# Gated mix of local attention and a Mish MLP: the second half's first layer by seven products, a joined v product, and GpSimd beside small softmax steps

## The chip, the core and the metric

The kernel runs on one core of one Trainium2 chip. The metric is device microseconds (us) of that core from one launch; the time of a kernel is the median of its runs, 620.25 us for the kernel before (three runs, 619.38 to 621.33). Engines are named as in the profile: PE (matrix multiply), PEld (its weight load), DVE (vector), ACT (scalar activation), POOL (GpSimd), SP (the queue that issues most transfers).

## The reference, cut to what matters

```python
x = A_x                                              # 2048 x 640, one batch
g = sigmoid((x * gate_w).sum(-1, keepdims=True))
q, k, v = split(x @ wqkv)                            # 32 heads of 20
# token s looks at s, s-2, ..., s-14 (8 positions, masked where negative)
a = softmax(q . k_window * 20**-0.5) @ v_window @ wo
h = x @ w1 + b1                                      # 640 -> 1728
b = (h * tanh(softplus(h))) @ w2                     # Mish, then 1728 -> 640
out = g * a + (1 - g) * b
```

All inputs are float32. The kernel keeps float32 accuracy on PE by splitting each operand into a rounded high part and a low part, so that one product of blocks is three matmuls (high by high, high by low, low by high: `mm3`, L515 to L517).

## The kernel before

**Tiling.** The 2048 tokens are four blocks `tb` of 512; blocks 0 and 1 are half P = 0, blocks 2 and 3 are half P = 1. The 640 input features are five K blocks `kc` of 128. The work on PE is, in order: the q, k, v projection in eight units `u` (half P, a quarter of the heads), each with eight slots of 15 matmuls; beside it the first MLP layer in six "quads" per half, a quad being two chunks of 128 hidden features by two token blocks, so four results of 128x512; then the second MLP layer (`mlp2`) and the output projection (`wo_part`).

**Products of blocks.** The first half's quads (`Quad`) use Strassen's scheme in Winograd's form on K blocks 0 to 3 (two pairs, seven products for eight), and K block 4 plainly. The intermediate sums are kept in PSUM: ACT copies a running sum from one bank to the next (`seed`, L1147), PE goes on adding to it, and for two of the four results DVE adds a kept product (`added`, L1165) before Mish. The second half's quads in the kernel before are `Plain`: four results, five K blocks each, no such copy and no such addition. A class `Single` is in the file too, but not used before: it takes one pair of K blocks (0 and 2) by seven products and the other three plainly.

**Operands.** `pieces(P, q)` loads the weights of a quad and splits them: ACT writes the high part (L447), then POOL or DVE the low part as a difference (L450). `x_forms(P, i)` builds the four sums of input blocks that the seven products need (L1020) and splits them. `sums_of` makes the same kind of sums of the second layer's weights (L1242, L1255).

**Attention.** It runs on DVE, two slots at a time: the product of q with k (`scores`, L572, 2560 elements per partition), its sum over a head (L575), the small softmax steps on 256 elements (largest L593, difference L594, sum L606, reciprocal L607, weights L608), the product with v (`outputs`, L617, two instructions of 1280 elements), its sum (L621), a transposition (L528).

**What sets the order.** `ORDER` is a list of tokens that creates the tasks (`u.4.3` is slot 3 of unit 4, `q.1.0.m1` a step of a quad, `pieces.1.0`, `sum`); `BANKS` says from which of two rings of three PSUM banks, `qb` or `sb`, a result takes its bank. A planner (`Plan.run`, L106) then walks through time with a cost for each task and writes each engine's instructions in the order that it finds; on the chip each engine runs its list in that order and waits on semaphores. For DVE and POOL it has a rule: POOL starts a task that can wait only while DVE runs a "quiet" one, and while POOL reads, DVE starts only quiet ones (`QUIET`, L72). Quiet are the large attention steps and tasks of kind `psum`. Before, the small softmax steps have no kind and so aren't quiet. Tasks marked "ANY" go to POOL or DVE, whichever the planner finds first.

Of the kernel before, what the change touches and what calls it, by code (L numbers as in the profile page):

```python
# [254 lines left out]
ORDER = """
u.0.5 u.0.7 u.0.6 pieces.0.1 q.0.0.first u.0.4 q.0.1.first q.0.0.second q.0.0.m1 q.0.0.m3 last.0 q.0.0.m4 q.0.1.m1 q.0.1.second q.0.1.m4 wq.1 q.0.0.m2
q.0.1.m3 last.1 q.0.0.l2 q.0.1.l2 u.1.1 q.0.0.l1 u.1.0 u.1.2 q.0.1.m2 u.1.3 u.1.4 u.1.7 pieces.0.2 q.0.1.l1 sum u.1.5 q.0.2.first q.0.2.m1 u.1.6
q.0.2.second q.0.2.m3 wa.2 p.2.1.a1 p.2.0.a1 q.0.2.m4 p.2.0.a2 pieces.0.3 sum q.0.2.m2 q.0.2.l2 p.2.1.a2 p.2.0.a3 p.2.0.b2 p.2.0.b1 p.2.1.a3 q.0.2.l1
p.2.2.a1 p.2.1.b1 p.2.2.a2 p.2.2.a3 p.2.2.b2 pieces.0.4 p.2.1.b2 p.2.3.a1 p.2.3.a2 p.2.2.b1 p.2.3.b1 p.2.3.a3 p.2.1.c0 wc.2 p.2.3.b2 x.3.4 q.0.3.first
p.2.0.c0 q.0.3.m1 q.0.3.second q.0.3.m3 q.0.3.m4 pieces.0.5 q.0.4.second q.0.3.l1 x.2.2 x.2.1 x.3.1 p.2.3.c0 q.0.3.m2 x.3.0 q.0.4.first q.0.3.l2  # L260
q.0.4.m1 p.2.2.c0 q.0.4.m3 q.0.4.m4 q.0.4.m2 q.0.4.l2 x.2.3 q.0.4.l1 q.0.5.first x.3.2 p.2.3.c1 x.3.3 wq.4 q.0.5.m1 q.0.5.second p.2.3.c2 q.0.5.m4
p.2.1.c1 p.2.2.c1 p.2.0.c1 p.2.0.c3 p.2.2.c2 q.0.5.m2 p.2.0.c2 p.2.2.c3 x.2.4 x.2.0 sum p.2.3.c3 q.0.5.m3 p.2.1.c3 q.0.5.l1 p.2.1.c2 q.0.5.l2
pieces.1.0 third u.4.2 u.4.3 u.4.5 u.4.1 u.4.4 u.4.7 u.4.0 u.4.6 rest.0 q.1.0.m1 rest.1 sum sum wq.5 q.1.0.m2 sum q.1.0.second pieces.1.1 pieces.1.2
q.1.0.first u.5.2 u.5.0 sum u.5.4 wq.6 u.5.1 pieces.1.3 u.5.7 q.1.2.second q.1.1.m2 u.5.5 u.5.3 u.5.6 q.1.1.second q.1.2.first sum u.6.3 q.1.1.m1
u.6.4 q.1.1.first q.1.2.m2 q.1.3.m2 u.6.1 q.1.3.m1 u.6.2 u.6.7 u.6.5 q.1.2.m1 lastw.1 u.6.6 u.6.0 pieces.1.4 sum last.2 wq.7 q.1.3.second q.1.4.m1
u.7.5 pieces.1.5 q.1.4.first q.1.4.m2 q.1.4.second q.1.5.second last.3 q.1.3.first u.7.0 u.7.7 u.7.4 q.1.5.m2 q.1.5.m1 q.1.5.first u.7.6 u.7.2 u.7.1
u.7.3 rest.2 rest.3
# [4 lines left out]
def kernel(ctx: ExitStack, tc: tile.TileContext, x, wq, wo, w1, b1, w2, out):  # L272
# [279 lines left out]
    def attention(u, P, hq, ready, gates):  # L552
# [36 lines left out]
        def softmax(a, rank, after, used):  # L589
# [3 lines left out]
            step("DVE", 430, lambda: V.tensor_reduce(mx[:, h], lg[:, h], op=OP.max, axis=AX.X), after)  # L593
# [9 lines left out]
        def shares(a, rank, e, copied):  # L603
            h = slice(a, a + 4)
            step = chain(rank)
            t = step("DVE", 415, lambda: V.tensor_reduce(sm[:, h], lg[:, h], op=OP.add, axis=AX.X), [e])  # L606
            step("DVE", 390, lambda: V.reciprocal(sm[:, h], sm[:, h]))  # L607
            return t, step("DVE", 430, lambda: V.tensor_tensor(pg[:, h], pg[:, h], sm[:, h, None, :].to_broadcast([128, 4, W, HQ]), op=OP.mult), [copied])  # L608

        def outputs(s0, rank, after):  # L610
# [3 lines left out]
            def mul(s):  # L614
                vw = window(kv, s0, 1)
                vw = bass.AP(tensor=vw.tensor, offset=vw.offset + s * ROW, ap=[list(vw.ap[0]), [2 * ROW, W // 2], [ROW, 2], [DH, HQ], [1, DH]])
                V.tensor_tensor(pairs[:, s].rearrange("p k i (h d) -> p k i h d", d=DH), vw,  # L617
                                pg[:, s0 + s].rearrange("p (k i) h -> p k i h", i=2)[:, :, :, :, None].to_broadcast([128, W // 2, 2, HQ, DH]), op=OP.mult)
# [1347 lines left out]
```

## Time and profile before

| | before |
|---|---|
| runs, us | 619.38, 620.25, 621.33 (median 620.25) |
| span of the profiled execution, us | 617.7 |
| PE busy | 611.9 us, 99%, 2716 instructions |
| DVE busy | 580.3 us, 94%, 546 instructions |
| ACT busy | 370.0 us, 60%, 856 instructions |
| POOL busy | 316.7 us, 51%, 291 instructions |
| TensorE clock granted | 0.999 of full |

The profiled execution gives its span, from the first to the last instruction; no other time stands for it, and the median of the runs is 2.55 us above that span. Matmuls are pipelined, and the busy time of one (0.39 us) is longer than the distance from one start to the next, so a busy PE says little about short gaps; the starts in the timeline do. Names of tiles: `sb` and `qb` are PSUM banks of the two rings, `pair` a split operand, `raw` a loaded one, `hb` an activation, `pr` the attention product, `lg` and `pg` logits and weights.

### The profile page before, as it was taken

The numbers are of one execution on the slowest core, as the hardware profiler recorded it, in microseconds if no ns is written. First come the engines' busy times: TensorE is split into PE (matmuls) and PEld (weight loads), VectorE is DVE, ScalarE is ACT, GpSimd is POOL, SyncE is SP. The second block draws the span as 40 slices with busy tenths as digits, with TensorE's granted clock in tenths as the row PEclk, the third lists the DMA queues.
The fourth block names the chain that finished last, engine by engine and source line by source line (L and its number), as shares of the span: only waits on it lengthen the run. The fifth ranks groups of instructions, "written<-read, shape, count | busy, mean of one in ns | idle before, by whom it ended". The sixth has DMA issues, their size and how long they took to land.

```text
span 617.7 us, 9122 instructions
## 1 busy us (share of the span) xinstructions
PE 611.9 (99%) x2716; PEld 508.1 (82%) x2716; DVE 580.3 (94%) x546; ACT 370.0 (60%) x856; POOL 316.7 (51%) x291
## 2 busy tenths in 40 slices
PE   9999999999999999999999999999999999999997
PEld 6878888888888888888888888888888888888886
DVE  8899999999999999999999999999989999989955
ACT  7685847677796456673465455777766543565520
POOL 1665758877865555745452737788427713001000
PEclk9999999999999999999999999999999999999999
DMA  9764775899997878898966859988869864599813
GB/s 330 227 184 146 197 254 167 242 294 263 337 303 229 252 238 253 227 282 281 236 187 222 233 175 286 304 219 259 261 219 285 241 211 131 178 327 295 305 53 119
DMA packets 100769, 145.95 MB, mean 236 GB/s; under 512 B 11552, under 2 KB 54560, under 8 KB 100496
## 3 DMA queue, kind: packets, MB, share of 16 engines
q1 hardware_dynamic: 97360, 139.61, 70.5%
q0 software_dynamic: 3072, 5.51, 6.0%
q8 instruction: 21, 0.34, 0.2%
q10 hardware_dynamic: 288, 0.26, 0.1%
q14 instruction: 28, 0.23, 0.1%
HBM read 91.33 MB, written 53.03 MB: 234 GB/s over the span
## 4 chain that ended last, share of the span: by engine, by line
PE 87%; DVE 7%; ACT 2%; DMA 2%; issue 2%; SPq 0%; DVEq 0%; ACTq 0%
PE qb L516 16%; PE qb L517 16%; PE qb L515 16%; PE sb L515 12%; PE sb L516 12%; PE sb L517 12%; DVE pr L572 2%; DVE lg L575 2%; DMA act<-hb 1%; DVE pair L450 1%; DVE raw L1020 1%; PE qb L677 1%; ACT hb L1153 1%; DVE hb L1165 1%; DMA ot<-o 1%
## 5 line engine op out<-in xcount | busy, mean ns | idle before, releaser
L450 POOL TENSOR_TENSOR pair<-raw,pair 128x512 fp32r<-128x512 f32 (+4 forms) x128 | 157.1, 1247 | 111.9 <-ACT pair L447 60.3
L447 ACT ACTIVATE pair<-raw 128x512 fp32r<-128x512 f32 (+2 forms) x229 | 132.8, 606 | 66.7 <-DMA raw<-actt 20.4
L517 PE MATMUL qb<-pair 128*128 128x512 f32 (+1 forms) x403 | 155.7, 386 | 0.0
L516 PE MATMUL qb<-pair 128*128 128x512 f32 (+1 forms) x403 | 155.7, 386 | 0.0
L515 PE MATMUL qb<-pair 128*128 128x512 f32 (+1 forms) x403 | 155.7, 386 | 0.0
L515 PE MATMUL sb<-pair 128*128 128x512 f32 (+2 forms) x374 | 144.9, 388 | 0.2
L517 PE MATMUL sb<-pair 128*128 128x512 f32 (+2 forms) x374 | 144.7, 387 | 0.0
L516 PE MATMUL sb<-pair 128*128 128x512 f32 (+2 forms) x374 | 144.7, 387 | 0.0
L617 DVE TENSOR_TENSOR pr<-kvq,pg 128x1280 f32<-128x1280 f32 x64 | 93.1, 1484 | 1.0
L572 DVE TENSOR_TENSOR pr<-kvq,qg 128x2560 f32<-128x2560 f32 x32 | 89.9, 2811 | 2.4 <-ACT qg L578 1.3
L621 DVE TENSOR_REDUCE kvq<-pr 128x320 f32<-128x2560 f32 x32 | 90.2, 2818 | 0.8
L575 DVE TENSOR_REDUCE lg<-pr 128x128 f32<-128x2560 f32 x32 | 90.2, 2818 | 0.7
L515 PEld LDWEIGHTS qb<-pair 128*128 128x128 f32 x403 | 75.6, 188 | 14.8
L516 PEld LDWEIGHTS qb<-pair 128*128 128x128 f32 x403 | 75.7, 188 | 14.7
L517 PEld LDWEIGHTS qb<-pair 128*128 128x128 f32 x403 | 75.6, 188 | 14.6
L515 PEld LDWEIGHTS sb<-pair 128*128 128x128 f32 x374 | 70.2, 188 | 15.3 <-ACT sb L1147 0.5
L516 PEld LDWEIGHTS sb<-pair 128*128 128x128 f32 x374 | 70.2, 188 | 14.1
L517 PEld LDWEIGHTS sb<-pair 128*128 128x128 f32 x374 | 70.2, 188 | 14.1
L450 DVE TENSOR_TENSOR pair<-raw,pair 128x512 fp32r<-128x512 f32 (+2 forms) x101 | 70.1, 715 | 2.6 <-ACT pair L447 2.3
L1020 POOL TENSOR_TENSOR hb<-hb 128x512 f32<-128x512 f32 x39 | 50.5, 1304 | 22.0 <-ACT hb L1153 12.7
L683 ACT ACTIVATE kvq<-qb 128x320 f32<-128x320 f32 x50 | 21.8, 436 | 50.1 <-PE qb L517 49.8
L447 ACT ACTIVATE pair<-hb 128x512 fp32r<-128x512 f32 (+3 forms) x62 | 36.5, 589 | 1.5 <-PE qb L517 1.2
(164 smaller groups left out, 730.3 us busy)
## 6 DMA issues: line engine op xcount, KB each, us to landing
actt<-hb SPq DMA_DIRECT2D x52, 256.0 KB, 3.8
raw<-in_w SPq DMA_DIRECT2D x40, 256.0 KB, 3.5
act<-hb SPq DMA_DIRECT2D x38, 256.0 KB, 3.0
raw<-actt SPq DMA_DIRECT2D x37, 256.0 KB, 3.7
raw<-in_wq SPq DMA_DIRECT2D x36, 248.0 KB, 3.8
raw<-act SPq DMA_DIRECT2D x29, 256.0 KB, 3.5
raw<-in_x SPq DMA_DIRECT2D x23, 256.0 KB, 4.6
o<-ot SPq DMA_DIRECT2D x64, 80.0 KB, 1.9
```

The lines of the kernel that those rows point to most:

```text
L447: a = add("ACT", act_ns(n), lambda: A.activation(hi(), raw(), AF.Copy), after, rank=rank, take=take, hold=hold)
L450: return (V if e == "DVE" else G).tensor_tensor(lo(), raw(), hi().bitcast(F32), op=OP.subtract)
L515: nc.tensor.matmul(ps, ah, bh, start=first, stop=False, skip_group_check=more)
L516: nc.tensor.matmul(ps, ah, bl, start=False, stop=False, skip_group_check=more)
L517: nc.tensor.matmul(ps, al, bh, start=False, stop=last, skip_group_check=more)
L572: return V.tensor_tensor(pr, window(kv, s0, 0), qg[:, :, None, :].to_broadcast([128, 2, W, QF]), op=OP.mult)
L575: V.tensor_reduce(lg_w[:, s0:s0 + 2], pr.rearrange("p s w (h d) -> p s w h d", d=DH), op=OP.add, axis=AX.X)
L617: V.tensor_tensor(pairs[:, s].rearrange("p k i (h d) -> p k i h d", d=DH), vw, pg[:, s0 + s].rearrange("p (k i) h -> p k i h", i=2)[:, :, ...
L621: V.tensor_reduce(q[:, s0:s0 + 2], pairs.rearrange("p s k i f -> p s f k i"), op=OP.add, axis=AX.XY)
L677: nc.tensor.matmul(ps.t[:, :n], X[0, kc].t[:, a, i * 128:(i + 1) * 128], WQ[0, kc].t[:, b, :n], start=a == b and kc == 0, stop=False)
L683: a = add("ACT", 330, lambda: A.activation(kv[:, 7 + s], ps.t[:, QF:3 * QF].rearrange("p (a b) -> p a b", a=2), AF.Copy), [done] + before, ...
L1020: return (V if e == "DVE" else G).tensor_tensor(t.t[:, i:i + n], a.t[:, j:j + n], b.t[:, k:k + n], op=op)
```

## The change

- All six quads of the second half become `Single`: one pair of K blocks by seven products, with `pieces` in its other branch and one `x_forms` for half 1 (the token `forms.1.0`).
- The product with v is one instruction for two slots in place of two.
- The five small softmax steps, the transpositions of the attention's output and of `hx`, and the DVE additions of `mlp2` get the kind `psum`, so that the planner lets POOL work beside them.
- Only matmuls that read the six kept input blocks now hold up the third attention buffer (`x_uses`).
- `ORDER` and `BANKS` are new throughout, the first half's part too.

```diff
-KIND = 'PPPPPP'
+KIND = 'SSSSSS'
-BANKS = {'q03al': 's', 'p23be': 'q', 'p21de': 's', ...}
+BANKS = {'l0': 's', 'p20al': 's', 'p20de': 's', ...}
-u.0.5 u.0.7 u.0.6 pieces.0.1 q.0.0.first u.0.4 q.0.1.first ...
-pieces.1.0 third u.4.2 u.4.3 u.4.5 u.4.1 u.4.4 u.4.7 u.4.0 u.4.6 rest.0 q.1.0.m1 rest.1 sum sum wq.5 q.1.0.m2 sum q.1.0.second ...
+u.0.5 u.0.6 u.0.4 u.0.7 q.0.0.first last.0 wq.1 q.0.0.m1 ...
+p.2.0.c2 u.4.3 q.0.5.l1 u.4.1 u.4.5 rest.0 u.4.2 sum pieces.1.0 forms.1.0 u.4.7 u.4.6 q.1.0.first u.4.0 q.1.0.m1 wq.5 u.5.4 ...
...
-            step("DVE", 430, lambda: V.tensor_reduce(mx[:, h], lg[:, h], op=OP.max, axis=AX.X), after)
+            step("DVE", 430, lambda: V.tensor_reduce(mx[:, h], lg[:, h], op=OP.max, axis=AX.X), after, kind="psum")
...
-            step("DVE", 390, lambda: V.reciprocal(sm[:, h], sm[:, h]))
+            step("DVE", 390, lambda: V.reciprocal(sm[:, h], sm[:, h]), kind="psum")
...
-            for s in range(2):
-                step("DVE", 1495, lambda s=s: mul(s), after if not s else (), kind="pv mul")
+            step("DVE", 2760, mul, after, kind="pv mul")
...
-        x_uses.append(add("PE", *a, **k))
-        return x_uses[-1]
+        t = add("PE", *a, **k)
+        if any(b.ring is plan.rings["xh"] for b in k["hold"]):
+            x_uses.append(t)
+        return t
```

What a quad of the second half now does (`Single`, there before but not called); `plain` stands for three K blocks:

```python
def first(self):   # al <- one product;  be <- copy of al
    self.p1 = self.mms(self.al, self.one(0, 0, self.xk(0, 0)), [], [self.al], True)
    self.sb = self.seed(self.be, self.al, [self.p1])
def second(self):  # ep <- one product;  v <- copy of ep
...
def m1(self):      # be += one product;  ga <- copy of be
def m2(self):      # al += one product + plain, then Mish
def m3(self):      # be += one product + plain, then DVE adds v, then Mish
def m4(self):      # ga += one product;  de <- copy of ga
def l1(self):      # ga += plain, then DVE adds v, then Mish
def l2(self):      # de += one product + plain, then Mish
```

More of the change, by code (lines that the diff above doesn't have):

```diff
@@ L255 @@
 ORDER = """
[L256 to L267, printed above, removed]
+u.0.5 u.0.6 u.0.4 u.0.7 q.0.0.first last.0 wq.1 q.0.0.m1 q.0.0.m4 q.0.0.m2 sum q.0.0.second q.0.0.m3 pieces.0.1 u.1.0 last.1 u.1.2 q.0.0.l2
@@ new lines @@
+p.2.2.c0 q.0.4.second q.0.4.m2 q.0.4.m4 p.2.1.b2 p.2.3.c0 p.2.3.b2 q.0.4.m3 wq.4 q.0.4.l1 q.0.4.l2 q.0.5.m1 p.2.0.c1 p.2.2.c1 p.2.3.c1 q.0.5.m2
+p.2.2.c2 x.2.3 q.0.5.m4 x.2.0 q.0.5.l2 q.0.5.second p.2.3.c2 p.2.0.c3 p.2.2.c3 p.2.3.c3 p.2.1.c1 p.2.1.c3 p.2.1.c2 x.3.2 third x.3.0 x.3.4 q.0.5.m3
+p.2.0.c2 u.4.3 q.0.5.l1 u.4.1 u.4.5 rest.0 u.4.2 sum pieces.1.0 forms.1.0 u.4.7 u.4.6 q.1.0.first u.4.0 q.1.0.m1 wq.5 u.5.4 rest.1 pieces.1.1 u.5.2
+u.4.4 q.1.1.first q.1.0.second sum q.1.0.m4 u.5.1 q.1.0.m3 u.5.3 sum q.1.1.second q.1.1.m2 sum u.5.6 q.1.1.m1 pieces.1.2 u.5.0 u.5.7 q.1.1.m4 wq.6
@@ new lines @@
+q.1.0.m2 u.5.5 q.1.2.first sum q.1.0.l2 u.6.2 u.6.4 q.1.1.l2 q.1.0.l1 q.1.2.m1 q.1.1.m3 u.6.3 wq.7 u.6.1 q.1.1.l1 u.6.5 u.6.0 u.7.2 u.6.7 u.7.3 u.7.6
+q.1.2.second q.1.2.m4 sum pieces.1.3 pieces.1.4 u.6.6 sum q.1.2.m2 q.1.4.first q.1.2.m3 q.1.2.l2 u.7.5 u.7.1 q.1.3.first q.1.3.m2 u.7.4 u.7.0
+q.1.3.second pieces.1.5 q.1.2.l1 q.1.3.m1 u.7.7 q.1.4.m1 q.1.4.m4 q.1.4.m2 q.1.3.m4 q.1.3.m3 q.1.3.l2 q.1.4.second q.1.3.l1 q.1.4.l2 rest.2
+q.1.5.first q.1.4.m3 q.1.5.m1 q.1.4.l1 q.1.5.m4 q.1.5.m2 lastw.1 q.1.5.second q.1.5.m3 q.1.5.l1 q.1.5.l2 last.2 last.3 rest.3
@@ L629, in out @@
             ot = plan.buf("ot", lambda: at.tile([128, QF // 32, 4, 32], F32, name="ot"))
-            t = add("DVE", 780, lambda: turn(ot.t, q[:, s0:s0 + 4], QF // 32), after, rank=rank, take=[ot])
+            t = add("DVE", 780, lambda: turn(ot.t, q[:, s0:s0 + 4], QF // 32), after, rank=rank, take=[ot], kind="psum")
             tb = 2 * P + (s0 == 0)
@@ L749, in ended @@
             kv = KV[UNIT[u]]
-            before = sum((freed.get((BEFORE.get(u), s), []) for s in range(8)), [])
+            before = sum((freed[BEFORE[u], s] for s in range(8)), []) if u in BEFORE else []
             halo = {}
@@ L1009, in mlp1_rest @@
         t = add("DVE", 430, lambda: turn(blocks(), hx[:, P, 4 * h:4 * h + 4].rearrange("p j a b -> p j (a b)"), FR // 32),
-                hxd[P] + before, rank=SOON, take=[z, b] if P else [b], late=late)
+                hxd[P] + before, rank=SOON, take=[z, b] if P else [b], late=late, kind="psum")
         d = turned_out(lambda: h_d[tb], blocks, [t], [b], late)
@@ L1409, in run @@
                 return (V if e == "DVE" else G).tensor_tensor(out.t, a.t, b.t, op=op)
-            return add(eng, either(eng, 512), run, after, rank=rank, take=take, hold=[out, a, b])
+            return add(eng, either(eng, 512), run, after, rank=rank, take=take, hold=[out, a, b], kind="psum" if eng == "DVE" else "")
         def result(b, tb, dc, after):
```

23 lines of the change are left out of this document (14 added, 9 removed).

## Prediction

> **What bounds the kernel now.** I read the page first, then a table of busy time by stage, then the starts of PE's matmuls one by one, then the groups of the engines that feed PE. The page's head:
>
> ```profile
> span 617.7 us, 9122 instructions
> PE 611.9 (99%) x2716; PEld 508.1 (82%) x2716; DVE 580.3 (94%) x546; ACT 370.0 (60%) x856; POOL 316.7 (51%) x291
> ```
>
> PE is the bound by share, with DVE close behind. A share can hide stages, so here are the stages: start-up, first half, second half's first layer (200 to 365 us), and the two output stages. The columns are PE, PEld, DVE, ACT and POOL, then the granted clock.
>
> ```profile
> core 0: us, PE busy (x) PEld busy (x) DVE busy (x) ACT busy (x) POOL busy (x), PEclk, DMA share, GB/s
> 0.00:62.00 62.00, 60.24 (x257) 47.78 (x257) 56.27 (x57) 42.73 (x100) 31.55 (x33) 1.00 0.68 221
> 62.00:200.00 138.00, 137.87 (x616) 115.50 (x617) 133.37 (x111) 98.15 (x248) 100.68 (x89) 1.00 0.83 256
> 200.00:365.00 165.00, 165.00 (x738) 138.33 (x737) 160.46 (x109) 89.23 (x229) 88.51 (x87) 1.00 0.80 239
> 365.00:420.00 55.00, 55.00 (x246) 45.85 (x246) 53.35 (x36) 38.05 (x84) 41.51 (x36) 1.00 0.81 244
> 420.00:500.00 80.00, 80.00 (x355) 66.24 (x354) 77.25 (x85) 52.28 (x107) 43.55 (x38) 1.00 0.86 255
> ```
>
> From 62 us on, PE is visibly idle for 0.13 us in all of these stages, at full clock. In the stage that changes, DVE is at 97% (160.46 of 165), but ACT at 54% and POOL at 54%. So a matmul less is time less, as long as PE's inputs and banks keep coming in time.
>
> What one matmul costs is read from starts, since its shown duration overlaps the next:
>
> ```profile
> 599.93 0.39 PE L515 MATMUL qb<-pair 128*128 128x512 f32 x1
> ...
> 611.26 0.39 PE L517 MATMUL sb<-pair 128*128 128x512 f32 x1
> ```
>
> Here are 50 steps of 128x512 in 11.33 us: **0.2266 us** each. (The Trainium skill, "TensorE: Matmul & The Clock Gate", section "Wait — 56ns, not 53.3ns?", gives 215.7 ns for a warm 512-wide step; by it the 18 matmuls below would be worth 3.9 us, not 4.1. The trace differs from it by 5%, and the trace decides.)
>
> With that step, all the gaps on PE behind the start-up can be found by their starts. There are three worth naming. The first:
>
> ```profile
> 35.01 0.39 PE L516 MATMUL qb<-kvq,pair 128*128 128x512 f32 x1
> 36.20 0.49 PE L517 MATMUL qb<-kvq,pair 128*128 128x512 f32 x1 [0.80 <-DVE pair L450]
> 36.53 0.39 PE L515 MATMUL qb<-kvq,pair 128*128 128x512 f32 x1
> ```
>
> 1.19 and 0.33 us where 0.23 each would do: 1.06 us lost, on a split that DVE made late. The second shows how the seven products stall:
>
> ```profile
> 57.92 2.82 DVE L572 TENSOR_TENSOR pr<-kvq,qg 128x2560 f32<-128x2560 f32 x1
> 60.66 0.68 DVE L1165 TENSOR_TENSOR hb<-hb,sb 128x512 f32<-128x512 f32 x1
> 61.37 0.58 ACT L1147 ACTIVATE sb<-sb 128x512 f32<-128x512 f32 x1 [1.74 <-DVE hb L1165]
> 61.49 0.39 PE L517 MATMUL qb<-kvq,pair 128*128 128x512 f32 x1
> 62.01 0.50 PE L515 MATMUL sb<-pair 128*128 128x512 f32 x1
> 62.34 0.39 PE L516 MATMUL sb<-pair 128*128 128x512 f32 x1
> ```
>
> The addition L1165 stood behind a 2.82 us attention product, the copy L1147 waited for the addition, and PE for the copy: 0.29 + 0.10 = 0.39 us lost. The third, at 177.56 us, is of the same family (the gap is 0.50 where a 496-wide step is 0.22, then 0.33):
>
> ```profile
> 174.11 2.81 DVE L575 TENSOR_REDUCE lg<-pr 128x128 f32<-128x2560 f32 x1
> ...
> 176.84 0.67 DVE L829 TENSOR_TENSOR sb<-sb,pair 128x496 f32<-128x496 f32 x1
> ...
> 177.06 0.38 PE L517 MATMUL qb<-pair,kvq 128*128 128x496 f32 x1
> ...
> 177.56 0.49 PE L515 MATMUL sb<-pair 128*128 128x496 f32 x1
> ...
> 177.89 0.39 PE L516 MATMUL sb<-pair 128*128 128x496 f32 x1
> ```
>
> Again 0.39 us. Together the three are 1.84 us, and none lies in the second half, where the plain quads have neither copy nor addition.
>
> **The change part by part.** *PE.* A plain quad is 4 results by 5 K blocks by 3 matmuls, 60. A `Single` has 3 in each of `first`, `second`, `m1` and `m4`, 12 in each of `m2`, `m3` and `l2`, and 9 in `l1`: 57. Six quads save 18 matmuls, all 128x512: 18 x 0.2266 = **4.08 us**. The order of the changed kernel has 18 PE rows fewer and no other difference in kind. No wider or narrower matmul comes in, so this term has hardly a range while PE stays the bound.
>
> *What feeds PE.* The rows of the groups (kept apart by shape; busy us, then mean ns of one):
>
> ```profile
> L617 DVE TENSOR_TENSOR pr<-kvq,pg 128x1280 f32<-128x1280 f32 x64 | 93.1, 1484 | 1.0
> L572 DVE TENSOR_TENSOR pr<-kvq,qg 128x2560 f32<-128x2560 f32 x32 | 89.9, 2811 | 2.4 <-ACT qg L578 1.3
> L450 DVE TENSOR_TENSOR pair<-raw,pair 128x512 fp32r<-128x512 f32 x88 | 62.7, 731 | 2.1 <-ACT pair L447 1.9
> L1165 DVE TENSOR_TENSOR hb<-hb,sb 128x512 f32<-128x512 f32 x12 | 8.2, 681 | 2.7 <-PE sb L517 1.4 <-ACT pair L447 0.8 <-ACT ot L635 0.6
> L607 DVE RECIPROCAL sm<-sm 128x32 f32<-128x32 f32 x16 | 5.6, 352 | 0.5
> ```
> ```profile
> L450 POOL TENSOR_TENSOR pair<-raw,pair 128x512 fp32r<-128x512 f32 x77 | 100.9, 1321 | 63.0 <-ACT pair L447 30.0 <-DMA raw<-in_wo 8.5 <-DVE hb L1020 5.5
> L1242 POOL TENSOR_TENSOR raw<-raw 128x128 f32<-128x128 f32 x9 | 4.7, 522 | 1.3 <-DVE pg L608 1.3
> ```
> ```profile
> L1147 ACT ACTIVATE sb<-sb 128x512 f32<-128x512 f32 x13 | 7.6, 587 | 5.8 <-PE sb L517 3.9 <-DVE hb L1165 1.7
> L447 ACT ACTIVATE pair<-raw 128x512 fp32r<-128x512 f32 x165 | 100.2, 625 | 54.3 <-DMA raw<-actt 20.4 <-PE qb L517 10.8 <-PE sb L517 10.1
> ```
>
> DVE: the joined product is not in the trace. Two rows bound it: two halves, 2 x 1484 = 2968 ns, if joining saves nothing, and 2811 ns by the q product, which has the same 2560 elements, an SBUF and a PSUM input and the same output. I take 2811, since 2811 less 1484 gives 1.037 ns an element, and 1280 more on 1484 is 2811 as well. That is 32 x 0.157 = 5.0 us less. Twelve additions L1165 come: 12 x 0.681 = 8.2 us. The order has 11 splits of 512 fewer on DVE: 11 x 0.731 = 8.0 us less; other differences there are single instructions. DVE is about 5 us lighter in all, hardly less than PE's own saving, so its share stays near 94%.
>
> POOL: 21 more splits of 512 and 23 small sums of 128x128: 21 x 1.321 + 23 x 0.522 = 39.7 us more, nearly all in the second half, since `pieces` and `x_forms` now make sums of weights and inputs. There POOL goes from 88.5 to some 125 us of 165, 76%. The first half's stage runs with 100.68 of 138, 73%, and loses only the 0.39 us shown. So I cost it at nothing; the cover is POOL's idle time, and if it were gone, a sum would come late by up to one split, 1.3 us. ACT: 24 copies, 24 x 0.587 = 14.1 us, and 10 more splits of 512, 6.3 us, in a stage where it is busy 54%. Transfers: 4 more on SP's queue, of which the small ones are 128x128; nothing.
>
> *Where the time can come back.* In ACT's list of the second half the copies now stand between splits. Before, at the first quad of the second half (`pair` and `raw` are weights of unit 5, `hb` the Mish results, `qb` and `sb` PSUM banks):
>
> ```order
> L689 ACTIVATE zt_77<-sb_2441 128x1
> L906 ACTIVATE zt_77<-zt_77 128x8
> L1153 ACT_TABLE_LOAD
> L1153 ACTIVATE hb_2527<-sb_2477,bias_75 128x512
> L578 ACTIVATE qg_273<-kvq1_269 128x320
> L447 ACTIVATE pair_2539<-raw_2495 128x496
> L1153 ACTIVATE hb_2560<-qb_2509,bias_75 128x512
> ```
>
> The same place in the changed kernel:
>
> ```order
> L1150 ACTIVATE sb_2500<-sb_2422 128x512
> L1150 ACTIVATE hb_2505<-qb_2468 128x512
> L448 ACTIVATE pair_2507<-raw_2385 128x496
> L448 ACTIVATE pair_2509<-raw_2392 128x496
> L448 ACTIVATE pair_2515<-raw_2401 128x496
> L448 ACTIVATE pair_2522<-raw_2460 128x496
> L1150 ACTIVATE qb_2539<-sb_2500 128x512
> ```
>
> PE now waits for ACT three times inside a quad (`be`, `ga`, `de`): nothing can be added to `qb_2539` until the last row has run, and four splits, each of which waits for its transfer, stand ahead of it. On DVE, the second addition of that quad in the changed kernel, between attention steps:
>
> ```order
> L623 TENSOR_REDUCE kvq1_269<-pr_274 128x320
> L573 TENSOR_TENSOR pr_274<-kvq1_269,qg_273 128x2560
> L1168 TENSOR_TENSOR hb_2505<-hb_2505,sb_2500 128x512
> L576 TENSOR_REDUCE lg_271<-pr_274 128x2x8x8
> L619 TENSOR_TENSOR pr_274<-kvq1_269,pg_272 128x8x2x160
> ```
>
> and before, at the same attention steps:
>
> ```order
> L621 TENSOR_REDUCE kvq1_269<-pr_274 128x320
> L572 TENSOR_TENSOR pr_274<-kvq1_269,qg_273 128x2560
> L575 TENSOR_REDUCE lg_271<-pr_274 128x2x8x8
> L617 TENSOR_TENSOR pr_274<-kvq1_269,pg_272 128x4x2x160
> ```
>
> The addition stands behind a 2.8 us product, just as at 60.66 us above; until it has run, bank `sb_2500` isn't free, and Mish behind it on ACT waits too. So the second half takes on the first half's kind of gap. Its price, from the gaps seen: two of 0.39 us in a first half that holds six quads and one projection unit of the same kind, 0.78 / 7 = 0.11 us each, six times: **0.7 us**. The bounds: below nothing, the new order could lose all three old gaps, 1.84 us; above, each of the 12 additions costs PE what it costs at 62 us when nothing covers it, 2.82 + 0.68 + 0.59 = 4.1 us, less the distance to the bank's next use, for which I take one slot of 15 matmuls, 3.4 us: 0.7 us, and as much again for a copy queued behind one split (0.625), so 12 x 1.3 = 16 us. I take 0.7, nearest to the rows seen. The old gaps I leave as they are.
>
> *The quiet softmax steps* cost DVE nothing, if POOL does not slow them. The trace has a case, and its opposite:
>
> ```profile
> 356.10 2.63 POOL L1020 TENSOR_TENSOR hb<-hb 128x512 f32<-128x512 f32 x2
> ...
> 358.28 0.42 DVE L593 TENSOR_REDUCE qg<-lg 128x32 f32<-128x256 f32 x1
> ```
> ```profile
> 27.02 1.30 POOL L450 TENSOR_TENSOR pair<-raw,pair 128x512 fp32r<-128x512 f32 x1 [1.13 <-ACT pair L447]
> 27.06 1.80 DVE L1020 TENSOR_TENSOR raw<-raw 128x512 f32<-128x512 f32 x1
> ```
>
> The step L593 ran wholly beside POOL in 0.42 us; a difference of two SBUF tiles beside POOL took 1.80, where the split of the same size has a mean of 0.73. Of the five steps none has two SBUF inputs. The reciprocal, SBUF to SBUF, is the doubtful one: it never ran beside POOL here. Bounds: nothing, or one POOL operation for each, 16 x 1.3 = 21 us of DVE. (The Trainium skill, "SBUF — State Buffer", section "Who interferes with whom", says the same of two inputs, and that the pair of ports is an exclusive lock, also against DVE's two-port modes; among the operations that enter these it lists copy, cast and tensor_scalar, not the reciprocal. The first part agrees with the two rows above; no run here shows the reciprocal.) I take nothing.
>
> The sum, on the profiled execution: 617.7 - 4.08 + 0.7 = 614.3 us. The runs' median lies 2.55 us above that span, so **616.9 us** as a median of runs.
>
> **The rivals.**
>
> *The gain is eaten.* The copies and additions cost 4 us instead of 0.7: six quads at 0.7 us, that is one handover in each of the kind at 62 us with no cover (4.1 less 3.4). For it: DVE at 97% in that stage, so an addition meets a 2.8 us step nearly always. Against: the first half does the same with DVE at 133.37 of 138, also 97%, at 0.39 us a gap. Time: 620.25 - 4.08 + 4.2 = 620.4.
>
> *It gets slower.* One mechanism: ACT's list. A copy that PE waits for stands behind splits, and each split behind its transfer; when one transfer is late, PE stops for the whole of it, and DVE's additions and the banks follow. Each quad has three such copies on PE's way (`be`, `ga`, `de`), 18 in all; at 0.4 us each, the size of the gaps seen, they cost 7.2 us: 620.25 - 4.08 + 7.2 = 623.4. It decides from 0.23 us a copy (4.08 / 18). For it: the 24 copies and four splits in a row above; PE's waits before are never for ACT in the second half, so nothing has tried it. Against: in the first half 24 such copies made one gap of 0.39 us.
>
> *The reciprocals block.* 21 us more on DVE; DVE has 617.7 - 580.3 = 37 us idle, of which half may cover: some 10 us on PE, 626. Little speaks for it.
>
> *The joined product saves nothing*, or POOL is not used beside the small steps: 5 us of DVE, inside DVE's idle time; the time stays 616.9 or so, within the forecast.
>
> **How the numbers follow.** A measurement of this kernel can tell about 0.3%, 1.9 us, from no change: faster is below 618.4, slower above 622.1. The forecast, with its own range of 614.3 (all old gaps gone too: 616.9 - 0.7 - 1.84) to 618.4, has 0.62. The gain eaten has 0.21, and of it I count all as "same". Slower by ACT's list 0.14, by the reciprocals 0.03. So faster 0.62, same 0.21, slower 0.17. The range reaches from 614.2 to 622.0: it leaves out the slower cases and a little below, about 2 in 10.
>
> **What would show it.** In the changed profile: 2698 PE instructions and the step still 0.2266; a span near 614.3. The joined product near 2.81 us; if 2.97, the term of DVE is wrong, but not the time. L608 (the reciprocal) at 0.35 us beside POOL. POOL busy near 356 us, ACT near 390, DVE near 575. Gaps between PE starts from 200 to 370 us: a sum near 0.7, ahead of them ACT copies behind DVE additions. I am wrong if these gaps sum to more than 3 us, or if a gap opens where `mlp2` begins (near 376 us), since the last quad now ends just ahead of it and its sums have to go out and come back.

## The result, and the profile after

The change is faster by 0.7%: a median of **615.92 us** (four runs, 615.07 to 616.89) against 620.10 us of the kernel before beside it (four runs, 619.38 to 621.33), a ratio of **0.9934** with an interval of 0.9918 to 0.9951. The difference of the medians is 4.18 us. Two runs of the experiments below, one with plain quads (885.55 us) and one of the kernel before beside it (769.02 us), had a granted clock of 0.657 and 0.753 and are left out here.

The head of the page after, with busy time, share and instructions of each engine:

```profile
span 615.1 us, 9163 instructions
PE 608.4 (99%) x2698; PEld 504.7 (82%) x2698; DVE 580.3 (94%) x517; ACT 386.4 (63%) x886; POOL 352.4 (57%) x334
```

PE has 18 matmuls fewer. DVE is as busy as before to the tenth of a microsecond, in 29 instructions fewer. The four runs took 615.07 to 616.89 us and their spans were 613.3 to 615.1: each run lies 1.8 us above its own span, and the profiled one is the longest of the four. The profiled execution of before, with the same 1.8 us, was one of about 619.5 us, shorter than its median. So the two spans, 617.7 and 615.1, understate the gain; the medians carry it.

The step of PE's matmuls is as before; two starts in the timeline after, 50 matmuls of 128x512 apart, give 11.33 us again:

```profile
597.17 0.39 PE L517 MATMUL qb<-pair 128*128 128x512 f32 x1
...
608.50 0.39 PE L516 MATMUL sb<-pair 128*128 128x512 f32 x1
```

The table of busy time by stage of the kernel after (columns as before: PE, PEld, DVE, ACT, POOL, granted clock, DMA share):

```profile
62.00:200.00 138.00, 136.50 (x607) 113.28 (x606) 131.28 (x93) 96.36 (x235) 107.78 (x94) 1.00 0.76 242
200.00:365.00 165.00, 165.00 (x740) 138.60 (x740) 161.11 (x107) 104.11 (x266) 103.07 (x111) 1.00 0.81 241
365.00:420.00 55.00, 54.27 (x240) 44.62 (x239) 53.94 (x39) 39.05 (x79) 42.61 (x37) 1.00 0.91 281
420.00:500.00 80.00, 80.00 (x355) 66.24 (x354) 78.38 (x72) 50.39 (x106) 51.79 (x46) 1.00 0.88 257
```

In the stage of the changed quads, 200 to 365 us, PE never stops although ACT went from 89.23 to 104.11 us and POOL from 88.51 to 103.07. What PE loses it loses ahead of that stage and just behind it. The starts of PE's matmuls, taken one by one with a step of 0.227 us for 512 columns and 0.220 for 496, give these gaps:

| gap on PE | before, us | after, us |
|---|---|---|
| start-up | 1.3 | 1.6 |
| 36.2 us, 45.0 us, 62.0 us | 1.06, 0.10, 0.39 | none |
| 147.2 us, 168.6 us | none | 0.40, 0.38 |
| about 177 us | 0.39 | 1.52 and 0.24 |
| 200 to 370 us | 0.0 | 0.0 |
| 374.0 us | none | 0.99 |
| sum | 3.5 | 5.3 |
| span less the sum | **614.2** | **609.8** |

The sum also holds gaps too small to list. The last row is what the kernel would take if PE never waited. It fell by 4.4 us: 4.08 for 18 matmuls, and 0.3 because the stretch behind the last matmul is shorter (3.6 us, 3.9 before). The gaps gave 1.8 us of that back in this execution. The largest gap is still in the first half; here the timeline of the kernel after (start, duration, engine, line, and in brackets the wait and what ended it):

```profile
175.30 0.39 PE L518 MATMUL sb<-pair 128*128 128x512 f32 x1
...
176.30 0.59 ACT L885 ACTIVATE qb<-pair 128x496 f32<-128x496 f32 x1 [1.89 <-DMA pair<-pu]
...
176.94 0.49 PE L516 MATMUL qb<-pair 128*128 128x496 f32 x1 [1.25 <-ACT qb L885]
```

ACT's copy L885 starts a bank of the projection (it reads a product of weights that was stored earlier and comes back as `pair<-pu`); it stood 1.89 us for that transfer, and PE stood for the copy. The other new gap is at the end of the quads; the same view:

```profile
370.04 0.44 ACT L579 ACTIVATE qg<-kvq 128x320 f32<-128x320 f32 x1 [1.03 <-DVE pr L573]
...
370.15 4.85 POOL L451 TENSOR_TENSOR pair<-raw,pair 128x512 fp32r<-128x512 f32 x4 [0.23 <-DVE pr L573]
...
371.47 1.28 ACT L1156 ACT_TABLE_LOAD   x1
...
372.76 0.69 ACT L1156 ACTIVATE hb<-sb,bias 128x512 f32<-128x512 f32 x1
...
372.87 0.39 PE L518 MATMUL qb<-pair 128*128 128x512 f32 x1
373.22 0.35 DVE L608 RECIPROCAL sm<-sm 128x32 f32<-128x32 f32 x1
373.35 0.59 ACT L1150 ACTIVATE hb<-qb 128x512 f32<-128x512 f32 x1
...
373.97 0.69 DVE L1168 TENSOR_TENSOR hb<-hb,sb 128x512 f32<-128x512 f32 x1 [0.39 <-ACT hb L1150]
373.99 0.50 PE L516 MATMUL qb<-pair 128*128 128x512 f32 x1 [0.73 <-ACT hb L1150]
```

PE needs a bank that holds a quad's kept product until ACT has copied it away (L1150, 373.35). That copy stands in ACT's list behind a Mish and the table load that the Mish needs, 1.28 + 0.69 us, and ahead of these ACT stood 1.03 us for an attention product of DVE (L579, 370.04), about as much as PE lost. So the handover of a copy does cost PE time, at one place out of six quads.

The groups of DVE by line and shape in the kernel after (busy us, mean ns of one, idle before):

```profile
L619 DVE TENSOR_TENSOR pr<-kvq,pg 128x2560 f32<-128x2560 f32 x32 | 90.2, 2820 | 1.0
L451 DVE TENSOR_TENSOR pair<-raw,pair 128x512 fp32r<-128x512 f32 x78 | 55.0, 723 | 2.4 <-ACT pair L448 2.1
L1168 DVE TENSOR_TENSOR hb<-hb,sb 128x512 f32<-128x512 f32 x14 | 9.5, 681 | 3.9 <-PE qb L518 2.0 <-DMA act<-hb 0.9 <-ACT hb L1150 0.4
L1168 DVE TENSOR_TENSOR hb<-hb,qb 128x512 f32<-128x512 f32 x10 | 6.8, 681 | 0.2
L608 DVE RECIPROCAL sm<-sm 128x32 f32<-128x32 f32 x16 | 5.6, 352 | 0.5
```

The joined product takes 2820 ns, 9 ns over the q product. The reciprocal keeps its 352 ns; the one at 373.22 above ran inside a stretch of four splits on POOL (from 370.15 us, 4.85 us long) and took 0.35 us.

### The profile page after: what moved, and what is told of

The parts are those of the page before. It is cut to its first block, busy times and chain, and to the rows that moved or that the text cites. A ratio compares the mean times of both kernels' runs of the same rounds, so it can differ in the third digit from the quotient of the medians.

```text
span 615.1 us, 9163 instructions
## 1 busy us (share of the span) xinstructions
PE 608.4 (99%) x2698; PEld 504.7 (82%) x2698; DVE 580.3 (94%) x517; ACT 386.4 (63%) x886; POOL 352.4 (57%) x334
## 4 chain that ended last, share of the span: by engine, by line
PE 93%; DMA 3%; DVE 1%; POOL 1%; issue 1%; ACT 0%; SPq 0%; DVEq 0%; POOLq 0%; ACTq 0%
PE qb L516 15%; PE qb L518 15%; PE qb L517 15%; PE sb L516 15%; PE sb L518 15%; PE sb L517 15%; DMA raw<-in_wq 1%; DMA pair<-pu 1%; DMA actt<-hb 1%; PE qb L680 1%; DVE pr L573 0%; POOL pair L451 0%; DVE lg L576 0%; POOL raw L1023 0%; PE sb L523 0%
## 5 line engine op out<-in xcount | busy, mean ns | idle before, releaser
L451 POOL TENSOR_TENSOR pair<-raw,pair 128x512 fp32r<-128x512 f32 (+3 forms) x142 | 178.0, 1282 | 84.5 <-ACT pair L448 48.2
L448 ACT ACTIVATE pair<-raw 128x512 fp32r<-128x512 f32 (+3 forms) x235 | 136.1, 611 | 49.6 <-PE sb L518 15.8
L516 PE MATMUL qb<-pair 128*128 128x512 f32 (+1 forms) x387 | 150.1, 388 | 2.0 <-ACT qb L885 1.3
L518 PE MATMUL qb<-pair 128*128 128x512 f32 (+1 forms) x387 | 150.0, 388 | 0.0
L517 PE MATMUL qb<-pair 128*128 128x512 f32 (+1 forms) x387 | 149.9, 387 | 0.0
L516 PE MATMUL sb<-pair 128*128 128x512 f32 (+2 forms) x384 | 148.4, 386 | 0.1
L518 PE MATMUL sb<-pair 128*128 128x512 f32 (+2 forms) x384 | 148.2, 386 | 0.0
L517 PE MATMUL sb<-pair 128*128 128x512 f32 (+2 forms) x384 | 148.2, 386 | 0.0
L573 DVE TENSOR_TENSOR pr<-kvq,qg 128x2560 f32<-128x2560 f32 x32 | 90.0, 2811 | 2.6 <-ACT qg L579 1.4
L619 DVE TENSOR_TENSOR pr<-kvq,pg 128x2560 f32<-128x2560 f32 x32 | 90.2, 2820 | 1.0
L516 PEld LDWEIGHTS qb<-pair 128*128 128x128 f32 x387 | 72.6, 188 | 17.1 <-ACT qb L885 1.7
L518 PEld LDWEIGHTS qb<-pair 128*128 128x128 f32 x387 | 72.6, 188 | 14.5
L517 PEld LDWEIGHTS qb<-pair 128*128 128x128 f32 x387 | 72.6, 188 | 14.4
L516 PEld LDWEIGHTS sb<-pair 128*128 128x128 f32 x384 | 72.1, 188 | 14.9 <-DVE sb L832 0.5
L517 PEld LDWEIGHTS sb<-pair 128*128 128x128 f32 x384 | 72.1, 188 | 14.2
L518 PEld LDWEIGHTS sb<-pair 128*128 128x128 f32 x384 | 72.1, 188 | 14.2
L451 DVE TENSOR_TENSOR pair<-raw,pair 128x512 fp32r<-128x512 f32 (+2 forms) x93 | 63.6, 705 | 2.8 <-ACT pair L448 2.4
L1023 POOL TENSOR_TENSOR raw<-raw 128x128 f32<-128x128 f32 (+3 forms) x58 | 45.4, 796 | 24.2 <-DMA raw<-in_w 11.6
L1023 POOL TENSOR_TENSOR hb<-hb 128x512 f32<-128x512 f32 x39 | 50.3, 1299 | 9.0 <-DVE lg L595 2.6
```

What stands on the lines that cost most here:

```text
L448: a = add("ACT", act_ns(n), lambda: A.activation(hi(), raw(), AF.Copy), after, rank=rank, take=take, hold=hold)
L451: return (V if e == "DVE" else G).tensor_tensor(lo(), raw(), hi().bitcast(F32), op=OP.subtract)
L516: nc.tensor.matmul(ps, ah, bh, start=first, stop=False, skip_group_check=more)
L517: nc.tensor.matmul(ps, ah, bl, start=False, stop=False, skip_group_check=more)
L518: nc.tensor.matmul(ps, al, bh, start=False, stop=last, skip_group_check=more)
L573: return V.tensor_tensor(pr, window(kv, s0, 0), qg[:, :, None, :].to_broadcast([128, 2, W, QF]), op=OP.mult)
```

## The experiments

The theory was that PE's number of matmuls sets the time and that join and quiet steps only take load off DVE. Its rivals were ACT's copies, which could eat the gain, and DVE's load, which could carry it. All times are medians, the ratios are to the kernel before as it was timed together with each (its medians were 619.5 to 620.1 us). "Without gaps" is the span less PE's summed gaps, as in the table above.

### The second half with plain quads

Everything of the change but the 18 matmuls:

```diff
-KIND = 'SSSSSS'
+KIND = 'PPPPPP'
```

> The changed kernel with plain products in all six quads of the second half and else nothing changed, so with the new order of tokens but 18 matmuls more. By the matmuls: 4.1 us above the changed kernel, 620. If the copies and additions of the seven products cost PE something that is hidden in the 615.9, then less than 4.1 above: the difference from 620 is their price.

Measured: 620.4 us (11 runs, 619.85 to 622.82; ratio 1.0016, 1.0004 to 1.0028), nothing less than before. The page:

```profile
span 618.9 us, 9115 instructions
PE 612.4 (99%) x2716; PEld 507.7 (82%) x2716; DVE 577.8 (93%) x518; ACT 373.7 (60%) x862; POOL 322.3 (52%) x295
```

So the join, the quiet steps, the looser hold on the third attention buffer, the new first half and the new order together gain nothing: the whole gain goes with the seven products. From here to the change it is 4.5 us, of which 18 x 0.2266 = 4.08 are matmuls; the remaining 0.4 isn't traced to one place. The span without gaps is 613.6, and the gaps are 5.3 us, as in the change. That matters, since the plan wrote new lists for this kernel too, and below such lists cost much more.

### Each copy of the second half twice

The 24 copies are emitted two times each, at an unchanged cost in the plan, so that every list keeps its order:

```diff
+            def run():
+                for _ in range(2 if self.P else 1):
+                    ins = A.activation(to.t, of.t, AF.Copy)
+                return ins
-            return add("ACT", 560, lambda: A.activation(to.t, of.t, AF.Copy), after, rank=-0.5, take=[to], hold=[to, of])
+            return add("ACT", 560, run, after, rank=-0.5, take=[to], hold=[to, of])
```

> The changed kernel with each of the 24 copies of running sums of the second half done twice, 0.59 us more each on ACT, with every list in the same order. If the order leaves slack around the copies (no gap stands from 200 to 370 us now), PE loses little: 616 to 617. If each copy on PE's way is just in time, 18 of them cost 0.59 us each: 626.5.

Measured: 617.88 us (12 runs, 615.59 to 622.85; ratio 0.998, 0.9959 to 1.0002). That is 2.0 us more than the change by the medians, 2.9 by the ratios, and the two intervals don't overlap. It is a little above the 616 to 617 that slack was to give, and far below 626.5. The page gives the work that was added, ACT's 398.9 us for 386.4:

```profile
PE 610.5 (99%) x2698; PEld 505.4 (82%) x2698; DVE 580.9 (94%) x517; ACT 398.9 (64%) x910; POOL 352.7 (57%) x334
```

So the time grows by 2.0 to 2.9 us for 12.5 us on ACT, 0.08 to 0.12 us for each of the 24 added copies; three quarters or more of them lie in slack. The profiled execution is one of the longer of the twelve, at 620.48. In it the gap behind the quads has grown by 0.6, one copy:

```profile
376.93 0.60 ACT L1152 ACTIVATE hb<-qb 128x512 f32<-128x512 f32 x1
...
377.58 0.49 PE L516 MATMUL qb<-pair 128*128 128x512 f32 x1 [1.29 <-ACT hb L1152]
```

From 200 to 370 us PE's gaps sum to 1.35 us, where the change has none. The largest of them, 0.87 us, doesn't end with a copy: PE waited for a low part that POOL made late, after 3.74 us of waiting for a transfer of weights.

```profile
325.52 1.00 POOL L1023 TENSOR_TENSOR raw<-raw 128x128 f32<-128x128 f32 x2 [3.74 <-DMA raw<-in_w]
...
327.82 0.50 PE L518 MATMUL sb<-pair 128*128 128x512 f32 x1 [0.60 <-POOL pair L451]
```

So not all of the 2.0 us is shown to be the copies' own. ACT's list is a real way to lose time here, but, with these lists, a small one.

### The join alone, two ways

First with the plan free to follow: the change without the join, and the kernel before with it. The diff of the first; the other is its mirror image.

```diff
-            def mul():
+            def mul(s):
...
-            step("DVE", 2760, mul, after, kind="pv mul")
+            for s in range(2):
+                step("DVE", 1495, lambda s=s: mul(s), after if not s else (), kind="pv mul")
```

> The changed kernel with the product with v as two instructions again: by the rows 32 x (2 x 1.484 - 2.820) = 4.7 us more on DVE. If PE's matmuls alone set the time, and DVE's idle time (35 us) covers it: 616, no change. If DVE is as much a bound as PE in its 97% stages, up to 4.7 us more: 618 to 621, with gaps on PE behind DVE.

> The kernel before with the joined product alone: some 5 us less on DVE, no matmul less. By the matmuls: 620, within 1 us of gaps. If DVE is a bound, down to 616.

Measured: the change without the join 629.31 us (6 runs, ratio 1.0143, 1.0118 to 1.0168); the kernel before with the join 644.20 us (5 runs, ratio 1.0386, 1.0362 to 1.041). Both lie far above every time that was expected. Removing it costs 13 us and adding it costs 24: that can't be the price of the instruction. PE's waits in the kernel before with the join, by what ended them (total, times, longest, us):

```profile
PE sb L515 <- DVE sb L829: 4.3, 2, 2.9
PE sb L515 <- ACT sb L1147: 2.1, 1, 2.1
PE sb L515 <- ACT sb L882: 1.8, 1, 1.8
PE qb L515 <- ACT hx L687: 1.7, 1, 1.7
```

No single culprit, but late sums, copies and bank releases in many places, 27.2 us of gaps in all. Without gaps both kernels stand where they should: 613.9 with 2716 matmuls, 609.6 with 2698. The cost of a task in the plan had changed, and with it every engine's list, while `ORDER` and `BANKS` had stayed. So the join was tried again with every list kept: in the change, two instructions inside the one planned task; in the kernel before, the joined instruction in the first of its two tasks and nothing in the second.

```diff
+            def both():
+                for s in range(2):
+                    mul(s)
-            step("DVE", 2760, mul, after, kind="pv mul")
+            step("DVE", 2760, both, after, kind="pv mul")
```

```diff
-            for s in range(2):
-                step("DVE", 1495, lambda s=s: mul(s), after if not s else (), kind="pv mul")
+            step("DVE", 1495, mul, after, kind="pv mul")
+            step("DVE", 1495, lambda: None, kind="pv mul")
```

> The changed kernel with the product with v as two instructions in the place of one, with all lists in the order of the changed kernel: 4.7 us more on DVE and nothing else. If DVE's length hardly matters and the earlier kernel without the join lost its time to another order, 616 to 617.5. If DVE is a bound, 618 to 620.6.

> The kernel before with the joined product in the place of the first of its two instructions and nothing in the second's, with all lists otherwise in the order of the kernel before: 5 us less on DVE and nothing else. If PE's matmuls are the bound: 619 to 620 (at most the gaps behind DVE go, 0.8 us). If DVE is a bound: 615 to 617.

Measured: the change with two products 616.81 us (12 runs, 615.43 to 620.25; ratio 0.9958, 0.9943 to 0.9974), not told apart from the change, since the intervals overlap. The kernel before with one product 619.90 us (12 runs; ratio 1.0009, 0.9997 to 1.0021): the same. With the order kept, the join is worth nothing that can be told: 0.9 us between the medians in the change, none in the kernel before. The page of the kernel before with the join says a second thing:

```profile
span 617.5 us, 9089 instructions
PE 611.7 (99%) x2716; PEld 508.0 (82%) x2716; DVE 581.4 (94%) x514; ACT 370.4 (60%) x856; POOL 317.2 (51%) x291
```

DVE has 32 instructions fewer than before and 1.1 us more to do. Its groups (busy, mean):

```profile
L618 DVE TENSOR_TENSOR pr<-kvq,pg 128x2560 f32<-128x2560 f32 x32 | 90.2, 2820 | 1.0
...
L450 DVE TENSOR_TENSOR pair<-raw,pair 128x512 fp32r<-128x512 f32 x88 | 64.8, 756 | 1.5 <-ACT pair L447 1.3
L450 DVE TENSOR_TENSOR pair<-hb,pair 128x512 fp32r<-128x512 f32 x34 | 24.1, 715 | 0.0
...
L1021 DVE TENSOR_TENSOR hb<-hb 128x512 f32<-128x512 f32 x9 | 7.3, 831 | 0.0
```

The product went from 93.1 to 90.2, 2.9 us less. The other three groups, splits and differences of two SBUF tiles, had 62.7 us in the kernel before, as shown ahead of the result, and in the same view:

```profile
L450 DVE TENSOR_TENSOR pair<-hb,pair 128x512 fp32r<-128x512 f32 x34 | 23.1, 684 | 0.0
...
L1020 DVE TENSOR_TENSOR hb<-hb 128x512 f32<-128x512 f32 x9 | 6.4, 728 | 0.0
```

From 62.7, 23.1 and 6.4 they went to 64.8, 24.1 and 7.3: 4.0 us more. One of them, with the POOL instruction beside it:

```profile
405.70 1.55 POOL L450 TENSOR_TENSOR pair<-hb,pair 128x512 fp32r<-128x512 f32 x1
```
```profile
406.08 1.72 DVE L450 TENSOR_TENSOR pair<-hb,pair 128x512 fp32r<-128x512 f32 x1
```

In the kernel before, eleven such DVE instructions took over 0.9 us, three of them behind 36 us; here there are fifteen, seven of them behind 36 us, and every one overlaps a POOL instruction. The four new ones, counted from 0.69 us, and one that grew from 1.11 to 1.58 us add 4.2 us, which is the growth. A product that is shorter than planned moves DVE against POOL, and in this list they meet more often. It isn't so in every list: in the change with two products DVE has 581.6 us, 1.3 more than with one.

### The quiet steps, and the halves

The change without the quiet kinds, and the kernel before with them (the five steps, the transpositions and the additions of `mlp2`; again with the plan free to follow, and the kinds are seen by the plan alone). One of the steps stands for all:

```diff
-            step("DVE", 390, lambda: V.reciprocal(sm[:, h], sm[:, h]), kind="psum")
+            step("DVE", 390, lambda: V.reciprocal(sm[:, h], sm[:, h]))
```

> The changed kernel without the quiet kind of the small softmax steps, so POOL does not begin beside them. If POOL's idle time covers it: 616. If POOL with its 40 us more needs these places, sums and splits come later, POOL's work goes over to DVE, and the time is 617 to 620.

> The kernel before with the quiet kinds alone: POOL may work beside the small steps; the steps themselves take 0.42 and 0.35 us as before. By the matmuls: 620, within 1 us. If POOL or DVE is a bound, 1 to 3 us less.

Measured: 649.45 us (6 runs, ratio 1.0482, 1.0455 to 1.0509) without them in the change, 632.05 us (4 runs, ratio 1.0195, 1.0175 to 1.0214) with them in the kernel before. Both expectations failed, both far on the slow side, though one run takes the kinds out and the other puts them in. One thing came as said: without the kinds the plan gives DVE work that POOL had, and DVE has 598.4 us for 580.3, with 103 splits of 512 from `raw` for 78. Without gaps the two stand at 609.6 and 613.9, so once more all of PE's loss is waiting. The largest gap of the change without them shows how a list goes wrong; first PE, then ACT's list ahead of it:

```profile
139.27 0.79 PE L516 MATMUL qb<-pair 128*128 128x512 f32 x1 [4.25 <-ACT qb L1150]
```
```profile
136.03 1.37 ACT L600 ACTIVATE pg<-lg,gate 128x64 f32<-128x64 f32 x4 [6.10 <-DVE pr L619]
137.34 0.61 ACT L448 ACTIVATE pair<-raw 128x512 fp32r<-128x512 f32 x1
137.86 0.28 ACT L688 ACTIVATE kvq<-qb 128x160 f32<-128x160 f32 x1
138.04 0.17 ACT L690 ACTIVATE hx<-qb 128x16 f32<-128x16 f32 x1
138.11 0.63 ACT L448 ACTIVATE pair<-raw 128x512 fp32r<-128x512 f32 x1
138.63 0.59 ACT L1150 ACTIVATE qb<-qb 128x512 f32<-128x512 f32 x1
```

A step of the softmax (L600) stood 6.10 us at the head of ACT's list for a DVE product; five instructions behind it was the copy that PE needed. It is the mechanism that the prediction gave to its slower rival, the head of ACT's list, only that DVE and not a transfer holds it, and in a list that fits its order badly.

Next, parts of the order were exchanged. The second half of before behind the new first half (with `KIND` plain), and the first half of before ahead of the new second half; `ORDER` and the entries of `BANKS` of one half are those of before, those of the other are the change's. Of the first of the two, the place where the halves meet:

```diff
-p.2.0.c2 u.4.3 q.0.5.l1 u.4.1 u.4.5 rest.0 u.4.2 sum pieces.1.0 forms.1.0 u.4.7 u.4.6 q.1.0.first ...
+p.2.0.c2 q.0.5.l1 pieces.1.0 third u.4.2 u.4.3 u.4.5 u.4.1 u.4.4 u.4.7 u.4.0 u.4.6 rest.0 ...
```

> The changed kernel with its new first half (order and banks), the joined product and the quiet softmax steps, but with the second half's order, banks and plain quads of the kernel before: 18 matmuls more than the changed kernel, as many as before. If the time goes by the matmuls alone (18 x 0.2266 = 4.1 us), it is that of before, 620 us within 1.5 us of gaps. If the new first half, the joined product or the quiet steps are what pays, it is at or below 618.

> The changed kernel with the first half's order and banks of the kernel before; the second half with its seven products stays as changed. By the matmuls: 616 us, within 1.5 us of gaps (the gaps at 36 and 62 us may come back, those at 147 to 178 us may go). If the new first half is what pays, 619 to 620.

Measured: the old second half 623.16 us (8 runs, ratio 1.0062, 1.0032 to 1.0091); the old first half 638.50 us (6 runs, ratio 1.0311, 1.0282 to 1.034). Both are slower than expected, the second by some 20 us. Without gaps 614.2 and 609.6, as their 2716 and 2698 matmuls want. So the new first half doesn't bring the gain, and the new second half brought it behind the first half for which it was ordered and not behind the old one. In the old second half one gap of 2.1 us stands out, again ACT behind DVE:

```profile
360.68 0.44 ACT L578 ACTIVATE qg<-kvq 128x320 f32<-128x320 f32 x1 [0.87 <-DVE pr L572]
361.06 0.28 ACT L687 ACTIVATE kvq<-qb 128x160 f32<-128x160 f32 x1
361.24 0.17 ACT L689 ACTIVATE hx<-qb 128x16 f32<-128x16 f32 x1
```
```profile
361.47 0.50 PE L515 MATMUL qb<-pair 128*128 128x512 f32 x1 [1.95 <-ACT hx L689]
```

Half of the quads as `Single`, nine matmuls fewer than before:

```diff
-KIND = 'SSSSSS'
+KIND = 'PPPSSS'
```

> The changed kernel with seven products in the last three quads of the second half only: 9 matmuls more than the changed kernel. By the matmuls: half way, 618.0 us. If the gain comes from somewhere else, it has no reason to lie there: either 616 or 620.

Measured: 653.24 us (4 runs, ratio 1.0535, 1.0518 to 1.0551), 35 us above what was expected. Without gaps 611.8: half-way between 614.0 and 609.6, as nine matmuls should be. The gaps are 39.6 us, one of them 17:

```profile
260.20 0.42 ACT L448 ACTIVATE pair<-raw 128x256 fp32r<-128x256 f32 x1 [6.94 <-DMA s<-raw]
...
260.67 0.79 PE L516 MATMUL qb<-pair 128*128 128x512 f32 x1 [16.95 <-ACT pair L448]
```

A split waited, by the profile, for a transfer that stores sums of weights (`s<-raw`), and PE for the split; the 6.94 us are only a part of PE's 16.95, and the rest of ACT's delay wasn't followed. This run says nothing about seven products; it says that this order was not made for three of them.

### The gap at 374 us

A try to close the gap behind the quads: the last result's bank from the other ring.

```diff
-BANKS = {'l0': 's', 'p20al': 's', ...}
+BANKS = {'l0': 's', 'l3': 's', 'p20al': 's', ...}
```

> The changed kernel with one result, the last of the first layer before the output stage, in a bank of the other ring; every engine's list keeps its order. In the changed kernel PE stops for 0.99 us at 374 us before that result, since its bank waits for a copy on ACT. If that reading is right, the gap goes and the time is 614.9. If PE meets another wait at once, 615.9, as without.

Measured: 616.17 us (6 runs, 615.39 to 617.16; ratio 0.9946, 0.9933 to 0.9959), the same as the change. The profile shows why: the result for which PE waits is the last but one, whose bank is still `qb`, so the wrong one was moved. The gap there is 0.49 us in this execution, 0.99 in that of the change, without a cause in the edit. Whether the right bank would win it wasn't tried.

### What the runs say together

| kernel | matmuls | median, us | gaps on PE, us | span without gaps, us |
|---|---|---|---|---|
| before | 2716 | 620.10 | 3.5 | 614.2 |
| before, one product, lists kept | 2716 | 619.90 | 3.5 | 614.0 |
| change, plain quads | 2716 | 620.4 | 5.3 | 613.6 |
| old second half | 2716 | 623.16 | 5.3 | 614.2 |
| before, quiet steps, new lists | 2716 | 632.05 | 17.1 | 613.9 |
| before, one product, new lists | 2716 | 644.20 | 27.2 | 613.9 |
| change, three of six quads | 2707 | 653.24 | 39.6 | 611.8 |
| **change** | 2698 | 615.92 | 5.3 | 609.8 |
| change, bank of the last result | 2698 | 616.17 | 4.9 | 609.6 |
| change, two products, lists kept | 2698 | 616.81 | 9.1 | 609.4 |
| change, copies twice | 2698 | 617.88 | 9.1 | 609.6 |
| change, two products, new lists | 2698 | 629.31 | 18.9 | 609.6 |
| old first half | 2698 | 638.50 | 26.4 | 609.6 |
| change, no quiet steps, new lists | 2698 | 649.45 | 35.4 | 609.6 |

The last column knows only the number of matmuls: 613.6 to 614.2, 611.8, 609.4 to 609.8. All else is in the gaps (the gaps are those of the profiled execution, which isn't always a median one).

## Why the prediction was right, and where it was not

**PE's term, 4.08 us: right.** 2698 instructions, a step still 0.227 us, and 4.18 us between the medians. It is the whole gain: with plain quads in the changed kernel the time is back at 620.4. The Trainium skill's 215.7 ns ("TensorE: Matmul & The Clock Gate", section "Wait — 56ns, not 53.3ns?") would make 3.9 us of it; the trace's step holds here too, though 0.2 us can't be told by the total.

**The gaps of the second half, 0.7 us: about the right size, in the wrong place.** From 200 to 370 us there is no gap at all, though 0.7 was expected there, by scaling the first half's gaps. The 0.99 us at 374 is a copy late in ACT's list, as was named, but behind a Mish, its table load and a wait for DVE, not behind splits. It sits at the end of the quads, where the prediction had said that a gap would show it wrong; by that sign it was wrong there, though the gap's reason is a bank and not sums that go out and come back. That the size nearly fits is luck. Why the copies inside the quads cost nothing isn't shown in detail; in the change they come in time, and the kernel with twice as many took 2 to 3 us more.

**The old gaps, left as they were: wrong in detail, harmless in sum by luck.** Those at 36, 45 and 62 us went, others came at 147 and 169, and the one at 177 grew from 0.39 to 1.76: 1.94 us in the first half and at its end before, 2.5 after. With an order that is new throughout, no single old gap should have been carried over by its place.

**The sum.** 614.3 was predicted as span and 615.1 came, but the profiled execution of after was the longest of its four and that of before a short one. The 2.55 us from span to median was two things: 1.8 us that every run has, and 0.75 by which the profiled execution of before was shorter than the median. The result of 615.92 lies 1.0 us below 616.9. An estimate, with the spans without gaps taken to hold for every run: at the medians PE's gaps are 620.10 - 1.8 - 614.2 = 4.1 us before and 615.92 - 1.8 - 609.8 = 4.3 after, so 0.2 us came where 0.7 was put; the rest is the shorter end (0.3) and a median of before that is 0.15 lower beside the change.

**DVE, 5 us lighter: wrong in a term, without consequence.** DVE has 580.3 us as before. The joined product costs what was taken, 2820 against 2811, but what it replaces was overstated: 64 x 1484 ns are 95.0 us, while the same row gives a busy time of 93.1, since instructions that follow each other overlap in the records. From busy to busy it is 93.1 - 90.2 = 2.9 us, not 5.0. The additions were right (9.5 + 6.8 - 8.2 = 8.1 us). The splits of 512 from `raw` fell by 7.7 (ten fewer, and one fewer from `hb`), but eight splits of 496 in place of five (1.6 us) and the larger input sums on L1023 (15.1 for 13.7) were left out. The result is near nothing.

**POOL and ACT: right in all, POOL's new work partly in another place.** POOL has 352.4 for 356, ACT 386.4 for 390; yet POOL stood at 62% in the stage of the quads, not 76%, as a part of the new work lies elsewhere (from 62 to 200 us it rose from 100.68 to 107.78, from 420 to 500 from 43.55 to 51.79).

**Quiet steps cost nothing: right.** The five steps have the same means as before, and the reciprocal, the doubtful one, takes 0.353 us on average in the six cases that lie wholly beside POOL and 0.352 in the six without it. By the Trainium skill ("SBUF — State Buffer", section "Who interferes with whom") an instruction with one SBUF input outside the two-port modes doesn't contend; the trace agrees, with these means, and shows the other side as well, the split of two SBUF inputs at 1.72 us beside POOL.

**The rivals.** "The gain is eaten" and "it gets slower" put six or eighteen handovers on PE's path; one came, of 0.99 us. Doubling the copies shows a price of at most 0.08 to 0.12 us for one copy more (0.11 to 0.16 if only the 18 on PE's way count), where the slower rival needed 0.4 and turned the sign at 0.23. Its mechanism is real nevertheless: in each of the six badly fitting orders an instruction of ACT is among PE's three longest waits, beside ones of DVE and POOL. "The reciprocals block" is refuted by the means. "The joined product saves nothing" came out nearest to true for the time, as it said.

**What the prediction did not see** is that the parts aren't separable. It costed each edit by itself and called join and quiet steps nothing; with lists kept, that holds for the join. With lists that the plan writes anew under the same `ORDER` and `BANKS`, taking out or putting in the join or the quiet kinds costs 12 to 34 us; taking out the seven products happened to fit, at 620.4. Since the quiet kinds act only through the lists, what they are worth by themselves stays open; the change's order was made with them, and without them the plan makes lists with 35.4 us of gaps from it. Which feature of an order makes a list bad was seen at the largest gaps, not settled in general.

## What to carry to other kernels

Where PE is at 99%, subtract its gaps, read from the starts, from the span: what is left follows the number of matmuls, and a change is worth its matmuls as long as the gaps stay. Where lists are written by a plan that was tuned for one set of costs, test a part with the lists kept; a part taken out with the plan running free measures the plan. And take differences of load from a row's busy time, not from its count times its mean.

## What was not expected of the hardware

In the kernel before with its lists kept, a shorter DVE instruction made DVE busier: 2.9 us saved on the product, 4.0 us added on splits and differences that then met POOL (one split took 1.72 us, in a group that had a mean of 0.684 before). In the change's lists the same exchange went the other way, 580.3 us with the join and 581.6 without. The switch of ACT's table cost its 1.28 us and nothing visible beside it: the load at 371.47 begins 0.02 us behind the split ahead of it in ACT's list and ends where the Mish starts, at 372.76. The Trainium skill ("ScalarE: Activation LUTs", section "What ACT_TABLE_LOAD costs") gives about the same for the load, 1.283 us, but adds a drain of 1.38 us to every switch; the rows here don't show that one.
